# Planning VectorE and GpSimd as engines that take turns, with one set of lengths for all stages

## The chip, the cores and the metric

The kernel runs on one core of a Trainium2 chip. The metric is the device time of one launch in microseconds, as the median of several runs. The core's engines work side by side, each through its own queue in program order: TensorE (PE: matmuls, with weight loads shown apart as PEld), VectorE (DVE), ScalarE (ACT), GpSimd (POOL), and SyncE (SP), which here issues most of the DMAs. An instruction that waits holds up all that stands behind it in its queue.

## The reference, cut to what matters

```python
# attention through 32 landmarks (4 x 8 heads, 576 tokens, 64 wide), then two feed-forward blocks
a = softmax(phi, axis=2)
k_m, v_m = a^T k, a^T v                      # einsum bhsm,bhsd->bhmd
attn = softmax(q k_m^T / 8); x = attn v_m    # heads side by side: 2304 x 512
x = ((x @ moe_w_a) * (x @ moe_w_b)) @ moe_w_out      # 512 -> 1536 -> 512
h = x @ moe2_w_in                                    # 512 -> 2048
out = (h * sigmoid(1.702 h)) @ moe2_w_out            # 2048 -> 512
```

All in 32 bits, to be met closely: `q` and `k` are scaled up, so the softmaxes are sharp.

## The kernel before, in words

**Precision.** Large operands are split into a high part, rounded by ScalarE to a matmul type (L349), and a low part, the difference (L343); each product is three matmul passes. This split is `hi_lo` (L346), and its subtraction goes through `combine` (L339), which also makes the sums and differences below. A `combine` has both inputs in SBUF and may run on VectorE or GpSimd. Evacuations of a PSUM bank have one input in PSUM and run on VectorE or ScalarE. The weights come as 64-bit floats and are decoded in place: two ScalarE passes (L445, L449) and one VectorE operation (L451).

**Stages**, by the trace. 0 to 105 us: attention (`memory`, `queries`, `softmax`), in which `warm_up` and `fill` keep PE running with matmuls of the identity (L1605) where the plan has nothing for it. Then, mixed with it and on to 240 us, `fold` multiplies the first block's weights with the landmark values (L798; out through ACT L818 and DVE L820 into `eff`), and `gated` makes the product of two matmul groups (L852; out through ACT L873 and DVE L876); `sum_tokens` (L892) prepares sums of it on GpSimd alone. 240 to 373 us: `project`, the product with `moe_w_out` as seven products instead of eight: for each of three thirds of the tokens and each product, three operands are loaded, split (128x768, into a ring of three slots) and used by 12 matmuls (L1014); a product's end goes out through DVE L1055. For the next stage `combine_tokens` and `combine_weights` then make seven operands from four (`seven`: four sums, seven splits; 384 and 256 wide). 373 to 548 us: `quad`, the seven products with `moe2_w_in` (L1290, out through DVE L1332). 548 to 592 us: `proj2`, the first 512 tokens with `moe2_w_out` (L1499), for which 16 parts of activations (512 wide, six slots) and the weights are split; beside it `load_pair` fetches eight pairs of weight tiles, issued from ScalarE's queue (L1462), and makes sums of them (256 wide). From 592 us: `proj2_seven`, the other tokens as seven products (L1530).

**What sets the order.** The program is written out by a planner, `Order` (L98). Streams ask for an engine with a ready time and a length in ns; the planner keeps a clock for each engine, and gives the engine to the stream that can start first, in steps of 40 ns, by priority among equals. Where two engines are offered, `_plan` takes the one that ends first, after adding a handicap: 300 for VectorE (`W0`, L22), so GpSimd gets an operation unless VectorE would end over 300 ns sooner. The lengths come from `dve`, `act`, `pool` (L79 to L88) and from the class `Lengths`, whose values are changed by stage: `measured` after the attention, `crowded` from `project` on (there a `combine` counts 1.3 times on GpSimd, 1.75 times on VectorE), `calm` and `short` later. Nothing of this runs on the chip: the lengths decide only in which order each queue's instructions stand, and on which engine.

## Time and profile before

| | us |
|---|---|
| median of 3 runs (740.36, 742.17, 742.63) | 742.17 |
| profiled execution: time, span | 740.76, 739.0 |
| PE busy in the span | 729.0 (99%) |
| VectorE, ScalarE, GpSimd busy | 535.2, 437.9, 294.1 |
| granted TensorE clock | 1.000 |

PE is almost never idle, so the time is the sum of PE's work and its few waits. For each wait one asks which engine ended it. A busy share of VectorE or GpSimd matters only in a stretch where PE waits for them.

### The profile page before, as it was taken

Reading aid. Unit: us, or ns where it says so; the run is one execution under the profiler, and the core shown is the slowest. Engines: PE = TensorE matmul, PEld = TensorE weight load, DVE = VectorE, ACT = ScalarE, POOL = GpSimd, SP = SyncE. Lnnn points to the kernel's source line nnn. Section 1 sums busy time; section 2 is a strip of 40 time slices with the busy share of each in tenths; the row PEclk is TensorE's granted clock in tenths of the full one; section 3 lists DMA queues with packets and bytes.
Section 4 is the critical chain, followed back from the end, with each engine's and each line's share of the span. In section 5 each row is a group of like instructions: output and inputs, shape, how many; then the busy total and the mean of one; then the engine's idle time right before and its main releaser. Section 6 shows DMA issues by size and latency. Waiting matters only on the chain.

```text
span 739.0 us, 14874 instructions
## 1 busy us (share of the span) xinstructions
PE 729.0 (99%) x5480; PEld 687.0 (93%) x5480; DVE 535.2 (72%) x910; ACT 437.9 (59%) x852; POOL 294.1 (40%) x278
## 2 busy tenths in 40 slices
PE   9999999999999999999999999999999999999997
PEld 8877888888889999999999999999998889999997
DVE  3988786568983447945999666676657988888774
ACT  3877664677873447547867676666555564444441
POOL 0414376458896616824998343233250000000000
PEclk9999999999999999999999999999999999999999
DMA  8999854886688875676536888875597474444411
GB/s 269 333 342 298 293 200 153 260 282 218 227 257 281 283 203 165 177 207 190 200 114 203 278 251 267 269 258 186 190 298 244 158 233 137 125 144 144 143 30 29
DMA packets 112600, 157.74 MB, mean 213 GB/s; under 512 B 8592, under 2 KB 89232, under 8 KB 112528
## 3 DMA queue, kind: packets, MB, share of 16 engines
q1 hardware_dynamic: 107168, 147.32, 62.8%
q10 hardware_dynamic: 5360, 9.47, 3.7%
q8 instruction: 43, 0.70, 0.4%
q14 instruction: 29, 0.24, 0.1%
HBM read 104.20 MB, written 52.56 MB: 212 GB/s over the span
## 4 chain that ended last, share of the span: by engine, by line
PE 89%; DVE 4%; DMA 4%; issue 1%; ACT 1%; SPq 0%; POOLq 0%; ACTq 0%; POOL 0%; DVEq 0%
PE bank L1290 22%; PE bank L852 21%; PE bank L1530 19%; PE bank L1014 16%; PE bank L798 3%; DMA raw<-w2d 3%; PE bank L1605 2%; PE bank L596 1%; DMA acc<-g2d 1%; DVE attn L343 1%; PE bank L514 1%; DVE w L343 1%; DVE acc L343 1%; PE bank L635 1%; PE bank L576 0%
## 5 line engine op out<-in xcount | busy, mean ns | idle before, releaser
L852 PEld LDWEIGHTS bank<-attn,eff 128*128 128x128 f32 x1152 | 154.2, 188 | 15.4 <-issue 5.2
L852 PE MATMUL bank<-attn,eff 128*128 128x288 f32 x1152 | 162.8, 298 | 0.0
L349 ACT ACTIVATE w<-acc 128x512 fp32r<-128x512 f32 (+2 forms) x144 | 83.9, 591 | 76.9 <-PE bank L1530 47.8
L1332 DVE TENSOR_TENSOR acc<-bank,acc 128x384 f32<-128x384 f32 x168 | 89.4, 552 | 46.4 <-PE bank L1290 30.9
L343 DVE TENSOR_TENSOR w<-acc,w 128x512 fp32r<-128x512 f32 (+2 forms) x122 | 83.0, 685 | 26.3 <-ACT w L349 26.0
L349 ACT ACTIVATE attn<-acc 128x768 fp32r<-128x768 f32 (+2 forms) x84 | 62.6, 752 | 54.9 <-PE bank L1014 38.9
L1014 PE MATMUL bank<-attn,w 128*128 128x384 f32 x504 | 91.9, 335 | 0.7 <-DVE attn L343 0.7
L343 DVE TENSOR_TENSOR attn<-acc,attn 128x768 fp32r<-128x768 f32 (+2 forms) x61 | 67.1, 1111 | 31.9 <-ACT attn L349 30.7
L1014 PEld LDWEIGHTS bank<-attn,w 128*128 128x128 f32 x504 | 87.6, 188 | 2.0 <-DVE attn L343 1.4
L1342 ACT ACTIVATE acc<-acc 128x384 f32<-128x384 f32 x96 | 48.4, 522 | 26.5 <-DVE acc L1332 25.7
L343 DVE TENSOR_TENSOR acc<-acc 128x512 f32<-128x512 f32 (+2 forms) x90 | 60.8, 686 | 0.8 <-POOL w1b L343 0.5
L1290 PE MATMUL bank<-attn,w 128*128 128x384 f32 x288 | 55.1, 334 | 0.0
L896 POOL TENSOR_TENSOR gr<-gr 128x288 f32<-128x288 f32 x48 | 44.2, 922 | 18.7 <-DMA g1d<-gr 8.2
L343 POOL TENSOR_TENSOR attn<-acc,attn 128x768 fp32r<-128x768 f32 (+1 forms) x22 | 37.7, 1726 | 34.6 <-ACT attn L349 34.6
L343 POOL TENSOR_TENSOR w<-dm,w 128x256 fp32r<-128x256 f32 x35 | 30.8, 894 | 51.2 <-ACT w L349 51.1
L1530 PE MATMUL bank<-attn,w 128*128 128x256 f32 x336 | 50.0, 284 | 1.0 <-ACT w L349 0.7
L1290 PEld LDWEIGHTS bank<-attn,w 128*128 128x128 f32 x288 | 50.4, 188 | 0.0
L1014 PE MATMUL bank<-attn,w1b 128*128 128x384 f32 x252 | 47.6, 336 | 0.2 <-DVE attn L343 0.2
L1290 PE MATMUL bank<-w1b,w 128*128 128x384 f32 x224 | 46.2, 334 | 0.0
L1530 PEld LDWEIGHTS bank<-attn,w 128*128 128x128 f32 x336 | 44.5, 192 | 1.4 <-ACT w L349 1.0
L1014 PEld LDWEIGHTS bank<-attn,w1b 128*128 128x128 f32 x252 | 43.9, 188 | 0.9 <-DVE attn L343 0.5
L1290 PE MATMUL bank<-w 128*128 128x384 f32 x224 | 43.8, 334 | 0.0
(172 smaller groups left out, 1374.7 us busy)
## 6 DMA issues: line engine op xcount, KB each, us to landing
acc<-g1d SPq DMA_DIRECT2D x63, 384.0 KB, 3.7
g2d<-acc SPq DMA_DIRECT2D x96, 192.0 KB, 4.1
acc<-g2d SPq DMA_DIRECT2D x14, 1024.0 KB, 6.4
raw<-in_moe_w_out_dram SPq DMA_DIRECT2D x24, 512.0 KB, 4.9
raw<-in_moe_w_in_dram SPq DMA_DIRECT2D x16, 512.0 KB, 5.1
g1d<-gr SPq DMA_DIRECT2D x12, 576.0 KB, 5.3
g1d<-acc SPq DMA_DIRECT2D x8, 576.0 KB, 4.8
raw<-in_moe_w_a_dram SPq DMA_DIRECT2D x16, 256.0 KB, 4.2
```

The costliest lines, as they stand in the source:

```text
L343: (nc.gpsimd if e == POOL else nc.vector).tensor_tensor(out=dst, in0=in0, in1=in1, op=op)
L349: nc.scalar.activation(out=hi, in_=src, func=AF.Copy)
L514: nc.tensor.transpose(ps[0][:, i * P:(i + 1) * P], qs[0][:, 2 * (c0 + i):2 * (c0 + i) + 2, :].rearrange("p e d -> p (e d)"), ident,)
L798: nc.tensor.matmul(ps[c][0][row(h), :], bdv[b][half, h, :], wt["wab", g, h][0][half, :], start=True, stop=True)
L852: nc.tensor.matmul(dst[:, :U], e[:, c, sw, i * CW + j * P:i * CW + (j + 1) * P], attn(b, mv, c, u * U, U), start=(n == 0), stop=(n == 3 * ...
L896: nc.gpsimd.tensor_tensor(out=dst, in0=in0, in1=in1, op=ALU.subtract)
L1014: nc.tensor.matmul(ps[0][:, :N2], w1_of(a, g, sw)[:, r * P:(r + 1) * P], b[0][:, mv, i], start=(first and q == n == 0), stop=(q == NG1 // ...
L1290: nc.tensor.matmul(ps[0][:, :N2], w[:, sw, r, :], y[mv][r], start=(n == 0), stop=(n == 5))
L1332: nc.vector.tensor_tensor(out=s[0], in0=ps[0][:, :N2], in1=x[0], op=ALU.add)
L1342: nc.scalar.activation(out=c[0], in_=c[0], func=AF.Gelu_apprx_sigmoid)
L1530: nc.tensor.matmul(ps[name][0][:, :NB], x[0][:, sw, c, :], moving(b, h // 2 + c, mv), start=(h == c == n == 0), stop=(h > 0 and c == K4 - ...
L1605: nc.tensor.matmul(ps[0][:, :P], ident, ident, start=True, stop=True)
```

## The change

The planner's model is replaced. `Lengths` and all that set it go (`measured`, `crowded`, `short`, `calm`); `dve` and `act` become fixed sums, 72 + n/0.96 and 100 (or 56 from PSUM) + n/1.2. A length may be marked `Held`: the planner keeps one more clock, `port`, and an operation with a `Held` length starts no earlier than the last `Held` one ended, on either engine. `Held` are both choices of `combine`, the decoding step L451, the GpSimd copy L545 and `sum_tokens`. The handicap for VectorE is -300 instead of 300. In the front part the planner reckons with loads at 335 bytes/ns that land 1700 ns later (300 and 2500 before), and with 110 ns instead of 70 for some transposes. The arithmetic is unchanged.

```diff
-W0 = 300.0
+W0 = -300.0
...
-FRONT = 1.0, 1.0, 1.0
-RATE0 = 300.0, 2500.0
+RATE0 = 335.0, 1700.0
...
+SIX = 798.0
...
-class Lengths:
-    dve, act, psum = 68, 94, 52
-    six, wide, three = 740, 2.54, 650
-    pool, both, slow = 1.0, 1.0, 1.0
...
-def measured():
-    Lengths.dve, Lengths.act, Lengths.psum = 150, 205, 160
-    Lengths.six, Lengths.wide, Lengths.three = 795, 2.71, 690
-    Lengths.pool, Lengths.both, Lengths.slow = 1.15, 1.4, 1.15
...
-def crowded():
-    measured()
-    Lengths.pool, Lengths.both, Lengths.slow = 1.3, 1.75, 1.55
...
-def dve(n, fast=False):
-    return Lengths.dve + n / (1.92 if fast else 0.96)
+class Held(float):
+
+    pass
+
+
+def dve(n):
+    return 72 + n / 0.96
 
 
 def act(n, psum=False):
-    return (Lengths.psum if psum else Lengths.act) + n / 1.2
+    return (56 if psum else 100) + n / 1.2
...
-        self.clock = {PE: 0.0, ACT: 0.0, DVE: 0.0, POOL: 0.0}
-        self.dma, self.marks, self.streams, self.count = 2000.0, {}, [], 0
+        self.clock, self.port = {PE: 0.0, ACT: 0.0, DVE: 0.0, POOL: 0.0}, 0.0
+        self.dma, self.marks, self.streams, self.count = 2800.0, {}, [], 0
...
-            t = max(self.clock[e], r[1])
+            t = max(self.clock[e], r[1], self.port if isinstance(d, Held) else 0.0)
...
             self.clock[e] = t + d
+            if isinstance(d, Held):
+                self.port = t + d
...
-        both = {POOL: Lengths.pool * pool(n), DVE: Lengths.both * dve(n)}
+        both = {POOL: Held(pool(n)), DVE: Held(dve(n))}
...
-        t, _ = yield DVE, t, slow * dve(512)
+        t, _ = yield DVE, t, Held(dve(512))
...
-            t, e = yield {POOL: 900, ACT: act(HG * C0 * M)}, max(t, et[1])
+            t, e = yield {POOL: Held(700), ACT: act(HG * C0 * M)}, max(t, et[1])
...
-            t, _ = yield POOL, t, Lengths.pool * pool(U)
+            t, _ = yield POOL, t, Held(pool(U))
```

**What it does to the queues.** The operations on PE, ScalarE and the DMA queues stay the same in kind, but for the identity matmuls L1605 (63 before, 56 now) eight small evacuations that go from ScalarE to VectorE, and two pairs of `gated` evacuations that are merged. Of the 530 `combine` operations 358 stood on VectorE and 172 on GpSimd; now it is 491 and 39. `sum_tokens` (96 operations) stays on GpSimd. In what follows the changed kernel's lines count lower: L328 is the old L343, L319 the old L334, L435 the old L451, L803 the old L820, L334 and L1435 on ScalarE the old L349 and L1462.

VectorE in `project`, at the second third of the tokens, before (`attn_83<-acc` is the split of an operand that PE waits for, 768 wide; `eff` and `acc`, 384 wide, are `combine_tokens` for the next stage):

```order
L343 TENSOR_TENSOR attn_83<-acc,attn_83 128x768 x4
L343 TENSOR_TENSOR acc<-acc 128x384
L343 TENSOR_TENSOR attn_83<-acc,attn_83 128x768 x2
L343 TENSOR_TENSOR acc<-acc 128x384 x2
L343 TENSOR_TENSOR eff<-acc,eff 128x384
L343 TENSOR_TENSOR attn_83<-acc,attn_83 128x768 x2
L343 TENSOR_TENSOR eff<-acc,eff 128x384
L343 TENSOR_TENSOR attn_83<-acc,attn_83 128x768 x3
```

Beside it GpSimd, before:

```order
L343 TENSOR_TENSOR eff<-acc,eff 128x384
L343 TENSOR_TENSOR acc<-acc 128x384
L343 TENSOR_TENSOR eff<-acc,eff 128x384 x2
L343 TENSOR_TENSOR acc<-acc 128x384
L343 TENSOR_TENSOR eff<-acc,eff 128x384
L343 TENSOR_TENSOR attn_83<-acc,attn_83 128x768
L343 TENSOR_TENSOR acc<-acc 128x384
```

The same place on VectorE now:

```order
L328 TENSOR_TENSOR attn_83<-acc,attn_83 128x768 x3
L328 TENSOR_TENSOR eff<-acc,eff 128x384 x2
L328 TENSOR_TENSOR acc<-acc 128x384
L328 TENSOR_TENSOR attn_83<-acc,attn_83 128x768
L328 TENSOR_TENSOR acc<-acc 128x384
L328 TENSOR_TENSOR eff<-acc,eff 128x384
L328 TENSOR_TENSOR attn_83<-acc,attn_83 128x768
L328 TENSOR_TENSOR acc<-acc 128x384
L328 TENSOR_TENSOR eff<-acc,eff 128x384
L328 TENSOR_TENSOR attn_83<-acc,attn_83 128x768
```

All 22 operations of that `combine_tokens` pair now stand on VectorE, two or three after each 768-wide split, and GpSimd has none of them.

VectorE in the attention, around the first `eff` evacuation, before (`sT` and `aT` are attention scores, `mx` and `sm` their small statistics):

```order
L343 TENSOR_TENSOR sT_112<-sT_112,sm_116 128x288
L676 STREAM_TRANSPOSE aT<-sT_112 128x288
L820 TENSOR_TENSOR eff<-bank,eff 128x512 x2
L676 STREAM_TRANSPOSE aT<-sT_111 128x288
L665 TENSOR_REDUCE sm_117<-sT_112 128x9
L562 TENSOR_REDUCE mx_106<-bank 128x1
```

The same place now:

```order
L328 TENSOR_TENSOR sT_112<-sT_112,sm_117 128x288
L328 TENSOR_TENSOR sT_112<-sT_112,sm_116 128x288
L328 TENSOR_TENSOR sT_111<-sT_111,sm_115 128x288
L660 STREAM_TRANSPOSE aT<-sT_112 128x288
L803 TENSOR_TENSOR eff<-bank,eff 128x512 x2
L328 TENSOR_TENSOR attn_83<-aT,attn_83 128x288
L660 STREAM_TRANSPOSE aT<-sT_111 128x288
L649 TENSOR_REDUCE sm_117<-sT_112 128x9
L546 TENSOR_REDUCE mx_106<-bank 128x1
```

Three operations that GpSimd had have joined VectorE's row.

ScalarE near the end of `proj2`, before (`w_1709<-acc 128x512` is a split of activations, the last of the 16 parts the one ahead of the row of six; the 256-wide rows are pairs of weights; L1462 issues a pair's load and waits until its buffer is free):

```order
L349 ACTIVATE w_1709<-acc 128x512
L1462 DMA acc<-w2d 128x2x512
L349 ACTIVATE w_1709<-raw_74 128x256 x3
L349 ACTIVATE w_1709<-acc 128x512
L349 ACTIVATE w_1709<-acc 128x256
L1462 DMA acc<-w2d 128x2x512
L349 ACTIVATE w_1709<-acc 128x256
L349 ACTIVATE w_1709<-acc 128x512
L349 ACTIVATE w_1709<-acc 128x256 x6
```

The same place now:

```order
L334 ACTIVATE w_1639<-acc 128x256 x4
L334 ACTIVATE w_1639<-acc 128x512
L1435 DMA raw_73<-w2d 128x2x512
L1435 DMA raw_74<-w2d 128x2x512
L334 ACTIVATE w_1639<-acc 128x512
L334 ACTIVATE w_1639<-raw_73 128x256 x2
L334 ACTIVATE w_1639<-acc 128x512
L334 ACTIVATE w_1639<-raw_73 128x256 x2
L334 ACTIVATE w_1639<-raw_74 128x256 x4
```

The eight pair loads now go to `acc`, `raw`, `acc`, `raw` by twos (before: `acc`, `acc`, `raw`, `acc`), and the last two are issued together, ahead of the last two splits of activations.

## Rows read from the trace of the kernel before

**Rows 1.** The page: the span, and part 1 for PE.

```profile
span 739.0 us, 14874 instructions
PE 729.0 (99%) x5480; PEld 687.0 (93%) x5480; DVE 535.2 (72%) x910; ACT 437.9 (59%) x852; POOL 294.1 (40%) x278
```

**Rows 2.** Busy time by stretch: stretch, length, engines, granted clock, DMA share, GB/s.

```profile
0.00:30.00 30.00, 28.64 (x365) 24.90 (x366) 17.56 (x52) 15.56 (x37) 4.40 (x11) 1.00 0.88 293
30.00:60.00 30.00, 27.51 (x316) 22.60 (x316) 26.48 (x60) 24.14 (x55) 9.48 (x11) 1.00 0.99 329
...
284.00:302.00 18.00, 17.56 (x99) 16.73 (x98) 17.27 (x12) 12.87 (x24) 17.42 (x12) 1.00 0.55 156
...
352.00:374.00 22.00, 21.49 (x123) 20.85 (x122) 21.43 (x21) 15.27 (x30) 22.00 (x17) 1.00 0.47 164
374.00:541.00 167.00, 167.00 (x965) 167.00 (x964) 121.95 (x213) 114.54 (x240) 78.49 (x86) 1.00 0.72 231
541.00:600.00 59.00, 57.81 (x287) 49.34 (x286) 44.56 (x102) 32.98 (x73) 6.59 (x5) 1.00 0.72 233
600.00:739.00 139.00, 135.03 (x1126) 134.83 (x1124) 107.25 (x193) 58.36 (x96) 0.00 (x0) 1.00 0.38 115
```

**Rows 3.** Timeline: start, length, instruction, in brackets idle time before and its releaser.

```profile
43.45 1.07 PE L514 MATMUL bank<-ident,q 128*128 128x128 f32 x8 [0.76 <-DMA q<-in_q_dram]
...
59.74 0.33 PE L514 MATMUL bank<-ident,q 128*128 128x128 f32 x1 [1.18 <-ACT qT L332]
...
296.64 4.11 PE L1014 MATMUL bank<-attn,w 128*128 128x384 f32 x22 [0.23 <-DVE attn L343]
...
301.31 0.98 PE L1014 MATMUL bank<-attn,w1b 128*128 128x384 f32 x4 [0.21 <-DVE attn L343]
...
366.90 0.65 PEld L1014 LDWEIGHTS bank<-attn,w 128*128 128x128 f32 x4 [0.81 <-DVE attn L343]
366.90 0.81 PE L1014 MATMUL bank<-attn,w 128*128 128x384 f32 x3 [0.49 <-DVE attn L343]
...
594.61 0.50 PE L1530 MATMUL bank<-attn,w 128*128 128x256 f32 x2 [0.75 <-ACT w L349]
```

**Rows 4.** VectorE's groups, 241 to 279 us, GpSimd mostly idle: count, busy us, mean ns.

```profile
L343 DVE TENSOR_TENSOR attn<-acc,attn 128x768 fp32r<-128x768 f32 x15 | 14.9, 993 | 14.2 <-ACT attn L349 13.8
L1055 DVE TENSOR_TENSOR acc<-bank,gr 128x384 f32<-128x384 f32 x6 | 3.3, 557 | 5.9 <-PE bank L1014 5.9
```

**Rows 5.** The same for 284 to 306 us, VectorE and then GpSimd.

```profile
L343 DVE TENSOR_TENSOR attn<-acc,attn 128x768 fp32r<-128x768 f32 x9 | 14.9, 1686 | 2.1 <-ACT attn L349 2.1
...
L343 POOL TENSOR_TENSOR eff<-acc,eff 128x384 fp32r<-128x384 f32 x6 | 8.8, 1478 | 5.6 <-ACT eff L349 5.6
```

**Rows 6.** Timeline: single operations with the other engine idle, and two back to back.

```profile
283.41 1.02 POOL L343 TENSOR_TENSOR eff<-acc,eff 128x384 fp32r<-128x384 f32 x1 [5.64 <-ACT eff L349]
...
294.34 0.55 DVE L343 TENSOR_TENSOR eff<-acc,eff 128x384 fp32r<-128x384 f32 x1
...
591.67 1.29 DVE L343 TENSOR_TENSOR w<-acc,w 128x512 fp32r<-128x512 f32 x2 [1.00 <-ACT w L349]
```

**Rows 7.** VectorE's groups, 352 to 374 us, and two of 30 to 60 us.

```profile
L1055 DVE TENSOR_TENSOR acc<-bank,gr 128x384 f32<-128x384 f32 x6 | 3.2, 550 | 0.6 <-PE bank L1014 0.6
...
L876 DVE TENSOR_TENSOR gr<-bank,gr 128x288 f32<-128x288 f32 x8 | 3.6, 454 | 2.4 <-PE bank L852 2.0 <-ACT raw_p L449 0.3
...
L343 DVE TENSOR_TENSOR attn<-aT,attn 128x576 fp32r<-128x576 f32 x1 | 0.7, 747 | 0.0
```

**Rows 8.** ScalarE's timeline, the chain of waits, the landing of L1462's loads.

```profile
583.22 0.37 ACTq L1462 DMA_DIRECT2D acc<-w2d  x1
583.63 1.55 ACT L349 ACTIVATE w<-acc 128x256 fp32r<-128x256 f32 x4 [1.05 <-DVE acc L343]
...
585.78 8.12 DMA acc<-g2d
...
DMA to landing us min/median/max: 3.6/4.7/7.3
```

More of the change, by code (lines that the diff above doesn't have):

```diff
@@ L54 @@
 )
-class Lengths:
-    dve, act, psum = 68, 94, 52
-    six, wide, three = 740, 2.54, 650
-    pool, both, slow = 1.0, 1.0, 1.0
-def measured():
-    Lengths.dve, Lengths.act, Lengths.psum = 150, 205, 160
-    Lengths.six, Lengths.wide, Lengths.three = 795, 2.71, 690
-    Lengths.pool, Lengths.both, Lengths.slow = 1.15, 1.4, 1.15
-def crowded():
-    measured()
-    Lengths.pool, Lengths.both, Lengths.slow = 1.3, 1.75, 1.55
-def short():
-    Lengths.dve, Lengths.act, Lengths.psum = 68, 94, 52
-    Lengths.pool, Lengths.both, Lengths.slow = 1.0, 1.0, 1.0
-def dve(n, fast=False):
-    return Lengths.dve + n / (1.92 if fast else 0.96)
+class Held(float):
+    pass
+def dve(n):
+    return 72 + n / 0.96
 def act(n, psum=False):
-    return (Lengths.psum if psum else Lengths.act) + n / 1.2
+    return (56 if psum else 100) + n / 1.2
 def pool(n):
@@ L168, in _plan @@
         if not isinstance(r[0], dict):
-            t = max(self.clock[r[0]], r[1] + (70.0 if r[0] == PE else 0.0))
+            t = max(self.clock[r[0]], r[1] + (70.0 if r[0] == PE else 0.0), self.port if isinstance(r[2], Held) else 0.0)
             return (t if len(r) < 4 else max(t, min(x[1] for x in r[3].free))), r[0], r[2]
@@ L441, in decode_piece @@
         mu = mf.bitcast(U32)
-        slow = Lengths.slow
         t, _ = yield ACT, t, act(512)
@@ L547, in memory @@
                 nc.scalar.activation(out=dst, in_=src, func=AF.Copy)
-        part = 240 if n < NHG else 70
+        part = 240 if n < NHG else 110
         t, ba = yield PE, t, part * last, bank_a
@@ L572, in memory @@
         nc.scalar.activation(out=et[0][:, last, :, 0], in_=even, func=AF.Exp, bias=m[2], accum_out=m[4])
-        t, _ = yield PE, t, 70 * last
+        t, _ = yield PE, t, 110 * last
         for c in range(last):
@@ L578, in memory @@
             )
-        t1, _ = yield PE, t2, 70
+        t1, _ = yield PE, t2, 110
         nc.tensor.transpose(bb[0][:, P:2 * P], et[0][:, last].rearrange("p s x -> p (s x)"), ident)
@@ L737, in close_attention @@
         pa.release()
-        measured()
         nonlocal py, pw
@@ L840, in gated @@
                 if not wide:
-                    t, ps = yield PE, t0, Lengths.six, bank_m
+                    t, ps = yield PE, t0, SIX, bank_m
                     dst = ps[0]
                 elif j == 0:
-                    t, ps = yield PE, t0, Lengths.six, pair_s
+                    t, ps = yield PE, t0, SIX, pair_s
                     dst = ps[0][:, j]
                 else:
-                    t, _ = yield PE, t0, Lengths.six
+                    t, _ = yield PE, t0, SIX
                     dst = ps[0][:, j]
@@ L1147, in room_kept @@
         give(f_s, views(acc, FN, 3, 2 * AN))
-    def calm():
-        for p in (1, 2):
-            for r in range(2):
-                yield "mark", "yc", p, r
-        measured()
     def room_projected():
-        od.spawn(9, calm())
         nonlocal p2
@@ L1176, in room_last @@
     def room_last():
-        short()
         alone[0] = True
@@ L1210, in room_last @@
             yield "mark", "wt", p
-        short()
         give(fw_s, views(acc, 2 * FN, 1))
@@ L1610, in main @@
         room_gated()
-        crowded()
         for p in range(NP):
@@ L1644, in tile_mem_attention_moe_moe2 @@
         n0 = 2 * NHG
-        measured()
-        Lengths.pool, Lengths.both, Lengths.slow = FRONT
         def loads():
```

## The prediction

> **What bounds the kernel now.** The page comes first: PE is busy for 729.0 of 739.0 us [rows 1], at the full granted clock in every stretch [rows 2]. PE's instructions stay as they are, so the change can move the time only by the 10 us in which PE is idle, by the identity matmuls that fill the front, and by waits that it adds. The table by stretch says where the idle time lies [rows 2]: 1.36 us in the first 30, 2.49 in 30 to 60, 0.44 in 284 to 302, 0.51 in 352 to 374, 1.19 in 541 to 600, and 3.97 at the very end, behind the last matmul. These add up to the 10 us, so from 60 to 284 and from 374 to 541 there is none: what VectorE does there is hidden, whichever engine has it. PE's timeline then names the releasers [rows 3]. In the front they are a load (0.76) and a ScalarE evacuation (1.18). In `project` all three are VectorE's 768-wide split (0.23, 0.21, 0.49). Near 594 us it is a ScalarE split (0.75).
>
> **Part 1: combines go from GpSimd to VectorE in `project`.** While GpSimd is mostly idle, a 768-wide split takes VectorE 993 ns [rows 4]; where GpSimd runs `combine_tokens` beside it, 1686 ns [rows 5]. So an operation that GpSimd takes over costs VectorE 0.69 us all the same, and done by VectorE itself it takes 0.55 us (384 wide, alone) [rows 6]. GpSimd needs 1.48 us for it there, 1.02 alone [rows 5, 6]. An evacuation from PSUM is not slowed: 550 ns in a stretch where GpSimd never rests, 557 where it does [rows 4, 7]. In these stretches GpSimd is no help to VectorE, and the two hold up the splits on which PE waits.
>
> Does VectorE alone keep up? In 284 to 306 us it would have nine splits (9 x 0.993 = 8.9 us) and the 22 operations of one `combine_tokens` pair (22 x 0.55 = 12.1): 21.0 us of 22. Back to back it is less: between 0.55 at 384 and 0.993 at 768 a 512-wide one lies at 0.70, yet two take 1.29 [rows 6], so 0.1 us of each overlaps the next; 31 operations then take 18 us. PE needs 12 matmuls at 167.00/965 = 0.173 us [rows 2] for each split, 2.08 us, or 18.7 us for nine, and the ring of three slots lets a split be up to two steps (4 us) early. It fits by the one count and nearly by the other, with two or three short operations between splits instead of one long one. I take these waits as gone. Their size: PE's idle time is 0.23 + 0.21 + 0.49 = 0.93 us, but the end of a pipelined matmul is modelled; the weight load before the third shows 0.81 instead of 0.49, 0.32 more, which for three gives 1.9. I take the middle, **-1.4 us**, with bounds -1.9 and 0.
>
> In 352 to 374 us, with the pairs of `combine_weights` beside the splits, both engines are full now: 21.43 and 22.00 of 22 us [rows 2]. VectorE alone: its own work without the six evacuations, (21.43 - 3.2) x 993/1686 = 10.7; the evacuations 3.2 [rows 7]; GpSimd's at 0.55 for 1.48 us, 8.2. That is 22.1 us of 22, or 18.3 with 0.1 of overlap for each of 38 operations. This is the tightest place of the change, and part of this work may run later, under `quad`, where VectorE is busy for 121.95 of 167 us [rows 2].
>
> A rule of the Trainium skill speaks against the move: Perfetto Trace Analysis, "Optimizing Scalar/DVE Operations", says that if VectorE is saturated, giving some of its work to other engines, even GpSimd, may make sense, and adds that the read port these two share may undo that. In this stretch the trace bears out the second half (993 against 1686 ns); by the first half the sum would hold +1 to +2 us here in place of the gain, and that is the slower rival below.
>
> **Part 2: the front.** Between the first and the third pair of `eff` evacuations VectorE gets four operations more of 288 columns and three of 576. Alone these take about 0.45 and 0.75 us [rows 7]: 4.0 us, less 0.7 of overlap 3.3. Evacuations that change places with ScalarE there about cancel (two wide ones fewer, four narrow ones more). VectorE has 30 - 26.48 = 3.5 us idle in 30 to 60 us [rows 2]: the work just fits, if the idle time lies where it is wanted. PE's waits there were ended by a load and by ScalarE, neither of which moves up much; the queue's new order may shift them. Bounds: -2.5 (all idle time closes) and +3.3 (none of VectorE's idle time can be used). I take **+0.2 us**, near the middle, since VectorE's new work meets its idle time. The seven identity matmuls fewer are worth nothing: they stand before the first `fold`, which waits for loads and decoding on ScalarE, and idle time takes their place.
>
> **Part 3: the end of `proj2`.** The chain of waits runs here through the last split of activations, which frees the buffer for a load of 8.12 us issued behind it (585.78), whose split is what PE waits for at 594.61 [rows 3, 8]. That split stood in ScalarE's queue behind the load of the last weight pair (L1462, issued at 583.22) and a 256-wide operation after 1.05 us of idle time [rows 8]. Now the last two pair loads are issued together, earlier, and the middle ones go to the raw buffers, so that they need not wait until the pairs before them are done with `acc`. Against it, two splits of the pair just loaded stand ahead of the last one, and such a load takes 3.6 to 7.3 us to land [rows 8]; before, too, the last but one pair stood so. If the last split comes 1.2 us earlier, PE's idle time of 1.19 us is gone [rows 2]; nothing more is to be had, because PE's own stream is late next. I take **-1.1 us**; bounds -1.2 and +2.6 (a pair load that takes the longest 7.3 us instead of the median 4.7).
>
> **Parts at nothing.** The fixed lengths and the load rates act only through the order. In `quad` VectorE gets most of GpSimd's 78.49 us [rows 2], at 0.55/1.48 of it some 29 us, less than its 45 us of idle time, and its evacuations from PSUM keep first claim by priority. If that cover were gone, each late evacuation would cost PE 0.55 us. In `gated` the sums stay on GpSimd.
>
> **Sum.** -1.4 + 0.2 - 1.1 = -2.3 us. Against the profiled execution's 740.76 that gives 738.5. This execution lies 1.4 us under the median of the three runs; carried over to the median, 742.17 - 2.3 = **739.9 us**. About 0.3%, 2.2 us, is what a measurement of this kernel can tell from no change, so the forecast lies on that edge.
>
> **The rivals.**
> - *The front closes too.* With ScalarE relieved of small evacuations its chain comes earlier, and PE's 2.49 us go as well: -1.4 - 2.5 - 1.1 = -5.0, 737.2 us. For it: 1.18 of the 2.49 us are ended by ScalarE [rows 3]. Against: the load at 43.45 has its own time.
> - *Gains and losses cancel.* VectorE, full in 30 to 60 us, delivers `eff` and scores about 1.5 us later, and the pair load lands late enough that the end of `proj2` gains little: -1.4 + 1.5 - 0.3 = -0.2, 742.0 us. For it: 3.3 us of work against 3.5 us of scattered idle time.
> - *VectorE becomes the bound* (slower). One mechanism, in 284 to 374 us and once in the front: the row of operations on VectorE is longer than PE's matmuls need, and GpSimd stands idle. It decides where VectorE's sum passes the stretch: 22.1 of 22 us by durations is that point, 18.3 by overlap is well below. Price: up to 22.1 + two late splits of 0.99 in 22 us is +2, and +3.3 in the front less what its idle time still takes, say +1.5: +3.5 in all with the end of `proj2` unchanged, 745.7 us. The rule named above is this case. Against it: in 284 to 302 us, where the trace has the two engines together, the same work takes longer than VectorE alone would need.
> - *The change doesn't act*: the order shows that it does, 133 combines change engine. That the turns are no turns is excluded by 993 against 1686.
>
> **How the numbers follow.** Forecast 0.45, the front closes too 0.15, cancel 0.25, VectorE the bound 0.15. Of the forecast's 0.45 two thirds lie beyond the 2.2 us, since its own bounds reach further down than up: 0.31 faster, 0.14 same. With 0.15 of the first rival, faster is 0.46; same 0.14 + 0.24 = 0.38; slower 0.15 + 0.01 = 0.16. The range takes in the first rival (737.2, less the 0.7 to the bound of part 1 and the rest of part 3: 736.5) and the lower part of the slower one: 744.3.
>
> **What would show it.** Right: no PE wait on the 768-wide split from 284 to 374 us; that split near 1.0 us there with GpSimd idle; VectorE's busy time higher in 30 to 60 and 284 to 374 us with PE's not lower; the last activation split ended before 583 us and no wait of PE behind 592 us. Wrong: PE waiting for VectorE between 352 and 400 us, or for `eff` or scores before 105 us, or ScalarE waiting for the last pair's load longer than 1.05 us.

## The result and the profile after

The changed kernel takes 745.68 us (median of 5 runs, 742.45 to 746.60); the kernel before, timed beside it, 740.50. The ratio is 1.0059, 95% interval 1.0038 to 1.0081; timed again later it was 1.0080 (1.0058 to 1.0102). So it is slower, by 4.4 and 5.9 us by the two ratios, which is small but clear of 1 by both intervals. Forecast was 739.9, with a range up to 744.3.

In code lines, the changed kernel's L328 and L334 are before's L343 and L349 (the two halves of a split), L781 and L835 its L798 and L852 (fold and gated), L997 its L1014 (projection), L1019 its L1036 (the copy that evacuates a product), L958 and L880 its L975 and L897 (loads of activations, stores of the gated sums), L1503 its L1530 (last stage).

Where did the time go? PE's instructions are the same except for seven identity matmuls, though in the front in another order, so the starts of its stages say it at once (us; two profiles of each kernel, the second ones from the experiments below):

| from the first matmul of ... to that of the next | before | before, again | after | after, again |
|---|---|---|---|---|
| start of the span to gated | 30.77 | 31.25 | 30.62 | 30.18 |
| gated (with attention and folds) | 208.77 | 208.87 | 211.51 | 213.26 |
| project | 133.72 | 133.75 | 135.75 | 135.35 |
| quad | 174.72 | 174.72 | 174.72 | 174.72 |
| proj2 | 43.71 | 43.56 | 43.56 | 43.56 |
| proj2_seven to the end | 147.29 | 146.97 | 147.73 | 148.52 |
| span | 738.98 | 739.12 | 743.89 | 745.59 |

Of the 4.9 us between the first profiles 2.74 arise in the gated stage and 2.03 in the projection. The quads, in which GpSimd's busy time falls from 78.49 [rows 2] to 25.65 us, agree to 0.01 us.

How much of it is waiting? PE's busy time over the gated stage before and after, then over the projection before and after (length, then PE, PEld, VectorE, ScalarE, GpSimd, clock, DMA share, GB/s):

```profile
30.77:239.54 208.77, 206.28 (x1980) 178.64 (x1979) 153.57 (x266) 138.01 (x281) 124.54 (x120) 1.00 0.78 257
30.62:242.13 211.51, 208.30 (x1981) 178.26 (x1979) 167.58 (x293) 137.39 (x277) 94.66 (x97) 1.00 0.77 256
239.54:373.26 133.72, 132.77 (x759) 130.91 (x758) 88.78 (x85) 77.12 (x125) 78.59 (x58) 1.00 0.66 199
242.13:377.88 135.75, 133.44 (x759) 132.51 (x757) 91.75 (x139) 77.83 (x127) 9.34 (x9) 0.99 0.67 197
```

In the gated stage PE's idle time grows by only 0.72 us (2.49 to 3.21); its busy time, for the same matmuls at the full clock, grows by 2.02. The page, and what PE waited for, by engine, tile and line, with the sum, the count and the longest wait in us (answers to [rows 1] and [rows 3]):

```profile
span 743.9 us, 14800 instructions
PE 730.1 (98%) x5466; PEld 686.1 (92%) x5466; DVE 563.4 (76%) x1049; ACT 431.8 (58%) x842; POOL 139.5 (19%) x145
```

```profile
PE bank L560 <- ACT et L552: 2.7, 2, 2.2
PE bank L997 <- ACT attn L334: 1.7, 1, 1.7
...
PE bank L1503 <- ACT w L334: 1.4, 1, 1.4
PE bank L541 <- DMA phi<-in_phi_dram: 0.7, 1, 0.7
PE bank L835 <- DVE eff L803: 0.4, 1, 0.4
```

The stretches of [rows 2], with 60 to 105 us added, and VectorE's 768-wide split and 384-wide operation in 284 to 306 us, which answer [rows 5] and [rows 6]:

```profile
30.00:60.00 30.00, 27.91 (x310) 21.66 (x309) 28.42 (x69) 23.04 (x52) 3.80 (x4) 1.00 0.97 321
60.00:105.00 45.00, 43.88 (x531) 36.08 (x531) 39.70 (x89) 31.27 (x78) 16.99 (x19) 1.00 0.82 274
284.00:302.00 18.00, 17.82 (x103) 17.86 (x104) 14.67 (x25) 13.78 (x26) 0.00 (x0) 1.00 0.64 180
...
352.00:374.00 22.00, 22.00 (x129) 22.00 (x128) 20.74 (x37) 18.16 (x34) 1.23 (x1) 1.00 0.71 225
374.00:541.00 167.00, 167.00 (x966) 167.00 (x965) 132.43 (x268) 109.94 (x236) 25.65 (x26) 1.00 0.67 223
```

```profile
L328 DVE TENSOR_TENSOR attn<-acc,attn 128x768 fp32r<-128x768 f32 x10 | 9.5, 954 | 3.0 <-ACT attn L334 2.7
L328 DVE TENSOR_TENSOR eff<-acc,eff 128x384 fp32r<-128x384 f32 x8 | 4.3, 551 | 0.3 <-ACT eff L334 0.3
```

So where the change was aimed at it does what it says: GpSimd is empty from 284 to 352 us, the split takes 954 ns instead of 1686, VectorE has 3.3 us to spare in 284 to 302 us, and PE's waits for it there are gone but for 0.2 us. The losses are elsewhere, at three places.

**261 us, in the projection.** The chain of waits (start, length, what) with ScalarE's timeline around it (start, length, instruction, in brackets idle time and its releaser):

```profile
254.44 0.36 SPq L958
...
254.89 6.46 DMA g1d<-gr
...
261.85 0.84 ACT attn L334
262.71 0.97 DVE attn L328
```

```profile
255.41 0.47 ACT L1019 ACTIVATE gr<-bank 128x384 f32<-128x384 f32 x1
261.46 0.49 ACT L1019 ACTIVATE gr<-bank 128x384 f32<-128x384 f32 x1 [5.58 <-DMA g1d<-gr]
```

ScalarE stands for 5.58 us at a copy into the storage "gr", until the store of the last gated block's sums, which reads that storage, has landed. The store was issued only at 254.89, behind a load on SP that waited for room, and took 6.46 us. Behind the copy, in ScalarE's queue, stand the splits that PE needs: it waits 1.70 us, then 0.37 for VectorE. Before, SP's last such store read another buffer:

```profile
251.32 0.36 SPq L897 DMA_DIRECT2D g1d<-acc  x1
```

Then the granted clock falls (PE alone: length, busy, clock, DMA share, GB/s):

```profile
260.00:262.00 2.00, 1.04 (x6) 1.00 0.49 182
262.00:264.00 2.00, 0.89 (x3) 1.00 0.00 0
264.00:266.00 2.00, 2.00 (x8) 0.55 0.51 135
266.00:268.00 2.00, 2.00 (x8) 0.59 0.99 313
268.00:270.00 2.00, 2.00 (x13) 1.00 0.63 175
```

After the idle time in 260 to 264 us PE runs for some 3.4 us at the lower level (0.50, 1.2 GHz), which loses 1.7 us more (0.45 and 0.41 of 2 us each): the waits of 2.07 us cost nearly twice their length. The first experiment has the sum.

**59 us, in the front.** The end of the chain of waits there, then PE's timeline around it, after and before:

```profile
57.99 0.68 DVE sT L328
58.70 0.68 ACT sT L647
59.38 0.97 ACT eff L801 x2
60.35 0.68 ACT et L552 x2
61.08 0.66 PE bank L560 x4
```

```profile
58.27 0.66 PE L498 MATMUL bank<-ident,q 128*128 128x128 f32 x4
61.08 0.66 PE L560 MATMUL bank<-ident,et 128*128 128x128 f32 x4 [2.16 <-ACT et L552]
```

```profile
59.83 2.62 PE L852 MATMUL bank<-attn,eff 128*128 128x288 f32 x18
...
62.83 0.60 PE L576 MATMUL bank<-ident,et 128*128 128x128 f32 x4
```

PE waits 2.16 us for ScalarE's exponential "et" (the longest wait there before is 1.18, for another evacuation [rows 3]). It stands in ScalarE's queue behind the exponential "sT", and that one waits for a subtraction on VectorE (57.99) which GpSimd did before. But "et" is not late: before, ScalarE began "sT" at 58.52 us instead of 58.70, and "et" at 61.21 instead of 60.24:

```profile
61.21 0.68 ACT L568 ACTIVATE et<-bank,mx 128x512 f32<-128x512 f32 x1
```

What differs is PE's own order. Before, PE had done 114 gated matmuls when it came to the transposes of "et" (L576, now L560), at 62.83 us and without a wait; now 96, so 18 that had covered the exponential stand behind it.

Before 105 us PE's gaps behind its first matmul add up to 4.21 us instead of 2.49; 0.7 of them in the first profile is a late load of phi. And PE's work is cut finer: 84 of the 1152 gated matmuls start 180 ns or more before the next (68 before), mostly 215 to 240 ns against 133 in a run, some 1.4 us of the 2.02 us of busy time above. The seven identity matmuls fewer are 1.1 us less of PE's work.

**599 us, ahead of the last stage.** PE waits 1.35 and 0.22 us: the last load of activations goes out 0.7 us earlier against PE than before (6.64 us ahead of the stage's first matmul, 5.91 before) but takes 8.87 us instead of 8.12 [rows 8]:

```profile
589.52 8.87 DMA acc<-g2d
```

### The profile page after: what moved, and what is told of

Its sections match the earlier page's. It is cut to its first block, busy times and chain, and to the rows that moved or that the text cites. A ratio compares the mean times of both kernels' runs of the same rounds, so it can differ in the third digit from the quotient of the medians.

```text
span 743.9 us, 14800 instructions
## 1 busy us (share of the span) xinstructions
PE 730.1 (98%) x5466; PEld 686.1 (92%) x5466; DVE 563.4 (76%) x1049; ACT 431.8 (58%) x842; POOL 139.5 (19%) x145
## 4 chain that ended last, share of the span: by engine, by line
PE 91%; DVE 4%; DMA 3%; ACT 1%; issue 1%; ACTq 0%; SPq 0%
PE bank L1263 23%; PE bank L835 21%; PE bank L1503 19%; PE bank L997 16%; PE bank L781 3%; PE bank L1472 3%; PE bank L580 1%; PE bank L1578 1%; DMA acc<-g2d 1%; PE bank L498 1%; DMA kv<-in_k_dram 1%; DMA g1d<-gr 1%; DVE w L328 1%; PE bank L619 1%; DVE attn L328 0%
## 5 line engine op out<-in xcount | busy, mean ns | idle before, releaser
L835 PEld LDWEIGHTS bank<-attn,eff 128*128 128x128 f32 x1152 | 154.4, 188 | 17.1 <-issue 6.0
L835 PE MATMUL bank<-attn,eff 128*128 128x288 f32 x1152 | 165.0, 298 | 0.4 <-DVE eff L803 0.4
L334 ACT ACTIVATE w<-acc 128x512 fp32r<-128x512 f32 (+2 forms) x142 | 82.7, 593 | 75.3 <-PE bank L1503 42.2
L328 DVE TENSOR_TENSOR w<-acc,w 128x512 fp32r<-128x512 f32 (+2 forms) x135 | 86.6, 648 | 27.2 <-ACT w L334 26.3
L328 DVE TENSOR_TENSOR attn<-acc,attn 128x768 fp32r<-128x768 f32 (+2 forms) x75 | 66.3, 896 | 38.5 <-ACT attn L334 37.5
L997 PE MATMUL bank<-attn,w 128*128 128x384 f32 x504 | 92.8, 339 | 2.3 <-ACT attn L334 1.7
L997 PEld LDWEIGHTS bank<-attn,w 128*128 128x128 f32 x504 | 89.1, 191 | 3.2 <-ACT attn L334 2.0
L334 ACT ACTIVATE attn<-acc 128x768 fp32r<-128x768 f32 (+2 forms) x80 | 61.0, 769 | 48.3 <-PE bank L997 42.4
L328 DVE TENSOR_TENSOR acc<-acc 128x512 f32<-128x512 f32 (+2 forms) x100 | 60.4, 624 | 0.1
L879 POOL TENSOR_TENSOR gr<-gr 128x288 f32<-128x288 f32 x52 | 49.4, 951 | 45.7 <-DMA g1d<-gr 21.4
L1503 PE MATMUL bank<-attn,w 128*128 128x256 f32 x336 | 50.0, 284 | 1.6 <-ACT w L334 1.4
L997 PE MATMUL bank<-attn,w1b 128*128 128x384 f32 x252 | 47.1, 334 | 0.0
L1503 PEld LDWEIGHTS bank<-attn,w 128*128 128x128 f32 x336 | 44.5, 192 | 2.0 <-ACT w L334 1.6
L997 PEld LDWEIGHTS bank<-attn,w1b 128*128 128x128 f32 x252 | 44.0, 188 | 0.0
L1503 PE MATMUL bank<-w 128*128 128x256 f32 x294 | 41.0, 283 | 0.0
L1263 PEld LDWEIGHTS bank<-w1b,w 128*128 128x128 f32 x224 | 39.5, 188 | 0.0
```

The source lines that it names most:

```text
L328: (nc.gpsimd if e == POOL else nc.vector).tensor_tensor(out=dst, in0=in0, in1=in1, op=op)
L334: nc.scalar.activation(out=hi, in_=src, func=AF.Copy)
L835: nc.tensor.matmul(dst[:, :U], e[:, c, sw, i * CW + j * P:i * CW + (j + 1) * P], attn(b, mv, c, u * U, U), start=(n == 0), stop=(n == 3 * ...
L879: nc.gpsimd.tensor_tensor(out=dst, in0=in0, in1=in1, op=ALU.subtract)
L997: nc.tensor.matmul(ps[0][:, :N2], w1_of(a, g, sw)[:, r * P:(r + 1) * P], b[0][:, mv, i], start=(first and q == n == 0), stop=(q == NG1 // ...
L1263: nc.tensor.matmul(ps[0][:, :N2], w[:, sw, r, :], y[mv][r], start=(n == 0), stop=(n == 5))
```

## The experiments

Kernels named a_ start from the changed kernel, those named b_ from the kernel before. Each one's median, its ratio to the kernel before, and its stages in us; "front" is first gated to first projection matmul (before 208.77, after 211.51).

| kernel | median | ratio (95%) | front | project | quad | span |
|---|---|---|---|---|---|---|
| a_place | 742.94 | 1.0035 (1.0015, 1.0055) | 214.14 | 131.57 | 174.72 | 740.25 |
| a_w0 | 752.73 | 1.0150 (1.0122, 1.0179) | 213.53 | 133.63 | 177.93 | 749.92 |
| a_noturn | 760.36 | 1.0255 (1.0230, 1.0280) | 217.22 | 142.89 | 176.86 | 759.14 |
| a_rate | 748.91 | 1.0093 (1.0074, 1.0113) | 218.73 | 131.55 | 174.72 | 747.13 |
| b_late | 745.12 | 1.0059 (1.0040, 1.0078) | 208.75 | 132.23 | 177.67 | 744.12 |
| b_w0 | 749.10 | 1.0122 (1.0101, 1.0142) | 214.03 | 132.33 | 178.62 | 748.15 |
| b_rate | 747.64 | 1.0102 (1.0084, 1.0120) | 210.30 | 136.76 | 174.78 | 744.74 |
| b_plain | 772.91 | 1.0437 (1.0411, 1.0464) | 227.25 | 139.35 | 182.23 | 770.70 |
| a_et | 743.93 | 1.0031 (1.0016, 1.0045) | 214.01 | 131.52 | 174.72 | 741.76 |
| a_again | 747.27 | 1.0080 (1.0058, 1.0102) | 213.26 | 135.35 | 174.72 | 745.59 |
| b_again | 740.91 (one run) | - | 208.87 | 133.75 | 174.72 | 739.12 |
| b_join | 739.81 | 0.9985 (0.9970, 1.0001) | 208.76 | 131.56 | 174.72 | 735.53 |
| b_join2 | 739.30 | 0.9975 (0.9963, 0.9987) | 208.74 | 131.57 | 174.72 | 737.69 |
| a_back | 752.27 | 1.0158 (1.0135, 1.0181) | 212.87 | 138.65 | 175.11 | 750.61 |

**a_place: other storage for the copies, same order.**

```
-        give(hc_s, views(p2_m, N2, 7))
+        give(hc_s, [views(p2_m, N2, 7)[i] for i in (0, 5, 6, 1, 2, 3, 4)])
```

> The changed kernel, with one difference: the seven 384-wide pieces of storage that the projection's copies use are handed out in the order 0, 5, 6, 1, 2, 3, 4, so that the second copy no longer goes where the last gated block's sums are still being stored. Order of instructions on every engine unchanged. Theory (the store holds the copy, the copy holds ScalarE, ScalarE holds TensorE, and the lower clock follows the wait): the projection gets 4.2 us shorter (first projection matmul to first quad matmul 135.75 us in the changed kernel, 131.5 here), no granted clock under 1.00 at 264 to 268 us, span near 739.7 us, ratio to the kernel before 1.000. Rival (the wait only shows where VectorE or the loads are late): TensorE waits again within 10 us, projection 134 to 136 us, ratio 1.004 to 1.006.

The projection took 131.57 us, 4.18 less (2.07 of waits, 1.7 of slow clock, 0.4 of PE's busy time besides), with the clock at 1.00 from 256 to 284 us: the wait for the store and what follows it are the whole loss there, and without them the projection is 2.15 us shorter than before:

```profile
244.76:376.33 131.57, 131.34 (x759) 131.05 (x758) 91.95 (x139) 78.16 (x127) 7.67 (x8) 1.00 0.67 199
```

The span is 0.5 us off what was expected, the ratio 0.0035. A part of that comes from the front, where this time the clock fell. PE's timeline and the clock there:

```profile
62.03 0.66 PE L560 MATMUL bank<-ident,et 128*128 128x128 f32 x4 [2.50 <-ACT et L552]
```

```profile
62.00:64.00 2.00, 1.97 (x12) 0.73 0.89 257
64.00:66.00 2.00, 2.00 (x10) 0.50 0.82 223
66.00:68.00 2.00, 2.00 (x46) 0.92 1.07 385
```

The order is that of the changed kernel, whose wait of 2.16 us left the clock at 1.00. Of a_place's ten runs four have a mean granted clock of 0.999 or more (741.39 to 742.89 us) and six 0.992 to 0.997 (742.03 to 748.01): the wait at 59 us lies where the clock falls in some executions and not in others. But the four at the full clock have a median of 742.5 us, still 1.6 above the kernel before beside them (740.88): the rest is the front's loss without a fall of the clock.

**a_w0, a_noturn, a_rate: one part of the change undone each** (preference; turns; arrival numbers).

```
-W0 = -300.0
+W0 = 300.0
```

```
-            if isinstance(d, Held):
-                self.port = t + d
```

```
-RATE0 = 335.0, 1700.0
+RATE0 = 300.0, 2500.0
...
-        part = 240 if n < NHG else 110
+        part = 240 if n < NHG else 70
```

> The changed kernel with the preference undone (W0 300 instead of -300, so that GpSimd takes more of the two-operand work); turns, plain lengths and arrival rates stay. If the preference for VectorE made the front longer (first gated matmul to first projection matmul 208.8 us before, 211.5 after), it is near 209 here and the span near 741; if turns or rates did, it stays near 211.5. The projection's wait for the store may go or stay, since the order of the gated blocks' buffers is drawn anew: projection 131.5 to 136 us. Ratio 0.998 to 1.006.

> The changed kernel without the turns (VectorE and GpSimd reckoned free of each other); preference, plain lengths and arrival rates stay. If turns made the front longer, first gated matmul to first projection matmul goes from 211.5 to about 209 us; if the preference or the rates did, it stays near 211.5. Where GpSimd gets work back, VectorE's 768-wide split beside it is long again (993 ns alone in the kernel before, 1686 beside), and TensorE waits for it again between 284 and 374 us, 0.9 us in all as in the kernel before. Ratio 0.998 to 1.006.

> The changed kernel with the arrival rates of before (RATE0 300 and 2500, first transfer at 2000, and 70 instead of 110 for a transpose); turns, plain lengths and preference stay. If the arrival numbers made the front longer, first gated matmul to first projection matmul goes from 211.5 to about 209 us and the 2.2 us that TensorE waits for an exponential at 58.9 us goes; if VectorE's load did, both stay. Ratio 0.998 to 1.006.

None brings the front back to 209 us; each makes it longer, by 2.0, 5.7 and 7.2 us. So no single part carries the front's loss: each undone part gives a new order with waits of its own. Two things can be read nevertheless. The store's wait at the first copies comes and goes with the order of the front: it holds ScalarE 5.0 us in a_w0 and 7.4 in a_noturn (PE waits 1.1 and 3.6 there), and it is not there in a_rate, whose projection takes 131.55 us. The clock fell behind the wait of 3.6 us in a_noturn (266.6 us) and behind one of 2.2 in a_rate's front (48.4), and not behind the 1.1 us of a_w0. And without turns PE waits for VectorE again in the projection, more than expected; its waits there:

```profile
PE bank L995 <- ACT attn L332: 3.6, 1, 3.6
PE bank L995 <- DVE attn L326: 3.5, 4, 1.9
```

**b_w0, b_rate, b_plain: one part done alone, from the kernel before** (the same lines the other way; for b_plain the three functions that set longer lengths do nothing).

> The kernel before with the preference alone (W0 -300 instead of 300). If preferring VectorE costs the front its 2.6 us, the first projection matmul comes at about 242 us instead of 239.5; if it does so only together with the rest, it stays within 1 us of 239.5. In the projection the reckoned prices of that stage (VectorE at 1.75) outweigh 300 ns, so some splits stay on GpSimd: projection 132 to 134 us. Ratio 0.998 to 1.006.

> The kernel before with the arrival numbers of the change alone (RATE0 335 and 1700, first transfer at 2800, 110 for a transpose). If these make the front later by themselves, the first projection matmul comes at about 242 us instead of 239.5; else within 1 us of 239.5. Projection about 133.7 us as before, unless the gated blocks' buffers come out in another order and the first copies meet the last store there (then 136 to 138). Ratio 0.998 to 1.008.

> The kernel before with plain lengths in all stages (72, 100 and 56 ns fixed, no factors), but no turns, no preference, and the arrival numbers of before. VectorE and GpSimd are then planned as if they did not disturb each other, while the trace of before shows the 768-wide split at 993 ns alone and 1686 beside GpSimd. If turns are what plain lengths need, the projection and the quads get waits for VectorE or GpSimd: projection 135 us or more, quads over 174.72 us, ratio over 1.005; if not, both stay, ratio 0.997 to 1.003.

All three are slower. b_w0's front is 5.3 us longer (1.7 of them from a fall of the clock at 62.7). b_rate's projection of 136.76 us lies in the range put down for copies that meet the last store, but not by that cause: ScalarE doesn't wait for the store there, and PE waits 2.9 us for GpSimd's splits and 1.4 for VectorE's. b_plain is the clearest: with plain lengths and no turns, PE waits for VectorE in folds, gated products, projection and quads:

```profile
PE bank L1010 <- DVE attn L339: 5.8, 5, 2.0
PE bank L848 <- DVE eff L816: 4.9, 6, 1.8
PE bank L1286 <- DVE acc L1328: 4.2, 6, 1.2
```

So plain lengths don't do without the turns (a_noturn says the same, at 1.0255). That the longer lengths of before were a rough way to the same end is a reading, which no run tests.

**b_late: only the projection's splits moved, in the kernel before.**

```
-        crowded()
+        crowded(); od.handicap[DVE] = -5000.0
         for p in range(NP):
             yield from project(p)
-        yield from quad(*order[0])
+        od.handicap[DVE] = W0; yield from quad(*order[0])
```

> The kernel before with one difference: during the projection alone (240 to 373 us) every split goes to VectorE; front, quads and tail are planned by the numbers of before, and TensorE's own order is that of before. Theory (of the change, the projection's part brings a gain by itself): the projection takes 131.6 us instead of 133.71, TensorE waits less than 0.3 us in it, the front stays at 239.5 us, span near 736.9 us, ratio 0.997. Rival (VectorE becomes the bound once it has all splits): waits for VectorE of over 1 us between 284 and 374 us, projection 134 us or more, ratio 1.000 or more.

The projection gained 1.5 us, as the theory had it, and VectorE did not become the bound. But the quads lost 2.95, more than that (PE waits 0.9 us for ScalarE and 0.9 for GpSimd in them, at another order), and the first gated matmul came 2.5 us late although the order up to there is that of before: phi's second transfer landed at 6.71 us instead of 4.77. PE's second row in that profile, beside that of b_again:

```profile
6.85 2.36 PE L557 MATMUL bank<-ident,phi 128*32 128x128 f32 x40 [1.29 <-DMA phi<-in_phi_dram]
```

```profile
5.50 2.11 PE L557 MATMUL bank<-ident,phi 128*32 128x128 f32 x40
```

**a_et: the wait at 59 us taken away.** On top of a_place, the exponential "sT" is planned behind "et":

```
-        t, _ = yield ACT, t, act(w)
+        t, _ = yield ACT, max(t, (yield "mark", "exp", 4)) if n == 3 else t, act(w)
```

> The changed kernel with the projection's storage handed out as in a_place, and one more difference: ScalarE's exponential for a block of scores (sT, at 58.7 us) is planned behind the exponential of phi's fifth block (et, at 60.2 us), for which TensorE waited 2.2 us in the changed kernel and 2.5 us in a_place. Theory (TensorE waits there because of ScalarE's order alone): the wait at 59 us falls to 0.5 us or less, no granted clock under 1.00 at 62 to 67 us, first projection matmul near 240 us (242.13 in the changed kernel, 244.76 in a_place), span near 736 to 738 us, ratio 0.995 to 0.999. Rival (VectorE, without a pause from 42 to 55 us, is late for what comes next): the wait moves on to the next scores or folds within 10 us, first projection matmul at 242 us or later, ratio 1.000 or more.

The wait shrank to 0.51 us and the clock stayed at 1.00, but the first projection matmul came at 244.10 us, as the rival had it. The rival's reason, VectorE, is not shown: from 60 us to the first projection matmul PE waits 0.4 us for VectorE and 2.4 for ScalarE, and PE's busy time in the gated stage is 210.32 us, 4.0 above before. A wait of 1.48 us has appeared at 144 us, where ScalarE decodes a piece that has just been loaded ahead of a gated evacuation; PE's and ScalarE's timelines:

```profile
144.64 1.60 PE L835 MATMUL bank<-attn,eff 128*128 128x288 f32 x10 [1.48 <-ACT acc L856]
```

```profile
142.84 0.66 ACT L429 ACTIVATE spare<-raw 128x512 f32<-128x512 f32 x1 [2.56 <-DMA raw<-in_moe_w_b_dram]
...
143.96 0.63 ACT L856 ACTIVATE acc<-bank 128x576 f32<-128x576 f32 x1
```

With the storage of a_place and this the kernel is 1.0031 (1.0016 to 1.0045): both waits gone, and still not under the kernel before.

**a_again, b_again: both kernels once more.**

> The changed kernel, unchanged, profiled and timed once more. By the theory the wait for the store at 261 us is there again, with about 4 us of granted clock at 0.50 to 0.69 behind it (projection 135.7 us). The wait at 59 us was 2.2 us without a fall of the clock in the first profile and 2.5 us with one in a_place: here either, the first projection matmul at 242 or at 244 to 245 us. Ratio 1.004 to 1.008.

> The kernel before, unchanged, profiled once more. What differs between its two profiles is the chip's own spread: if the second transfer of phi (landed at 4.77 us in the first profile, 6.71 in the kernel with the projection alone moved) is late here too, the first fold comes at 28 to 29.6 us instead of 27.14 and the front is up to 2.5 us longer with the same instructions; if not, the stages agree within 0.3 us, span 739.

The kernel before repeats within 0.6 us in every stage, with the same waits. The changed one has all its waits again, and this time the clock fell at both: at the end of 2.5 us at 59 us and behind 1.3 and 0.4 at 262.

**b_join, b_join2, a_back: front and back exchanged.** b_join is the kernel before with the change's turns, plain lengths and preference switched on ahead of the first projection matmul; a_back is the changed kernel with the numbers of before from there. PE's order is that of the kernel whose front it has. In b_join's edit, plain() sets 72, 100 and 56 ns without factors for all that follows and switches the turns on:

```
+        plain()
+        od.handicap[DVE] = -300.0
         room_gated()
-        crowded()
```

> The kernel before up to the first projection matmul (every engine's order there as before), and from there the change's reckoning: turns, plain lengths, VectorE preferred. TensorE's order is that of before all through. Theory (the change is a gain behind the front, and its loss lies in the front and in one wait for a store): front 239.5 us, projection 131.6 to 132.2 us, quads 174.7, then 43.6 and 141.3 to 143.4; span 735 to 737.5, ratio 0.994 to 0.998. Rival (the back of the changed kernel only fits its own front): waits in the quads as in the kernel with the projection alone moved (quads 177.67 us there), span 740 us or more, ratio 1.000 or more.

> The counterpart of b_join: the changed kernel up to the first projection matmul (every engine's order there as changed), and from there the reckoning of before (the longer lengths, no turns, GpSimd preferred). TensorE's order is the changed kernel's. If the change's front loses by itself, the first projection matmul comes at 242 to 244.8 us again; if its back gains by itself, this kernel also loses what b_join won there: projection 133 us or more with waits for VectorE between 284 and 374 us, quads 174.7 or more; span 743 to 750, ratio 1.005 to 1.012. If the wait for the store at 261 us comes from where the front leaves its buffers, it may be here too (projection 135.7 us or more, the clock down behind it); if it comes from the order in which loads and that store are issued behind the front, it is gone, since here the store stands ahead of the load. Rival (front and back gain or lose only as a pair): front within 1 us of 239.5, or projection near 131.6.

> The kernel b_join (front of before, reckoning of the change behind it) profiled and timed once more, over more rounds. Its first profile had a span of 735.5 us and its timed runs a median of 739.8 us. If the gain behind the front is steady (projection 131.56, quads 174.72, 43.56 and 141.97 us in the first profile) and only the front and the wait ahead of the last stage vary, those four stages come out within 1.5 us in sum here, and the ratio is 0.996 to 0.999. Rival: some runs have a wait in the quads or a fall of the clock, which the first profile did not show; then the quads exceed 174.8 us here or the ratio is 1.000 or more.

These four corners say which half loses:

| | back of before | back of the change |
|---|---|---|
| front of before | 1 | 0.9985 (0.9970, 1.0001), 0.9975 (0.9963, 0.9987) |
| front of the change | 1.0158 (1.0135, 1.0181) | 1.0059 (1.0038, 1.0081), 1.0080 (1.0058, 1.0102) |

The front loses by itself (212.87 us in a_back, 1.7 of them from a fall of the clock), and the back gains by itself: the projection is 131.56 and 131.57 us, 2.15 under before, with quads at 174.72. In a_back ScalarE stands for 4.81 us at the same copy, so the wait for the store comes from where the front leaves its buffers. Its projection has the old waits and more, VectorE's split at 1446 ns beside GpSimd in 284 to 306 us:

```profile
260.07 0.49 ACT L1055 ACTIVATE gr<-bank 128x384 f32<-128x384 f32 x1 [4.81 <-DMA g1d<-gr]
```

```profile
PE bank L1033 <- POOL attn L362: 2.9, 3, 1.5
PE bank L1033 <- DVE attn L362: 1.7, 3, 0.8
```

b_join2's two middle stages repeat b_join's, but proj2 and the last stage are 2.1 us longer in sum, more than the 1.5 expected: PE waits 1.3 us for ScalarE's "w" ahead of the last stage, which b_join did not. The two don't add up: behind the front of the change its own back is 5 to 7 us better than the old one, behind the old front 1 to 2. By the second ratio the kernel that joins the old front to the new back is faster than the kernel before, by 0.13 to 0.37%, and so than both.

## Why the prediction was wrong

**Part 1, the projection: right in mechanism, a little short in size.** -1.4 us was put down, with -1.9 as its bound; without the store's wait it is -2.15 (131.57 against 133.72). VectorE alone kept up: 14.67 us of 18 in 284 to 302 us and 20.74 of 22 in 352 to 374, against the 18.3 to 22.1 that the prediction reckoned for the second. Two thirds of the gain is not idle time in the profile: in a_place PE's idle time in the projection falls by 0.72 us against before and its busy time by 1.43, which the prediction had suspected when it put the bound at -1.9. The 0.55 us of [rows 6] was not read alone, since GpSimd ran beside that operation from 294.50 us; with GpSimd empty it is 551 ns, so the term stands. The rule of the Trainium skill weighed there (Perfetto Trace Analysis, "Optimizing Scalar/DVE Operations", that giving VectorE's work to other engines may help when it is saturated, unless the shared port undoes it) is borne out in its second half again: 954 ns with GpSimd empty, 1446 with it busy in a_back.

**The step that failed first is one that was not made: the sum held no term for buffers.** The prediction followed operations between engines and looked for waits of PE on VectorE in 284 to 374 us. The 4.2 us came at 261 us, from a copy on ScalarE behind a store, because the reordered front leaves its last sums in the storage that the projection's first copies overwrite. a_place, which changes only that storage, shows it. It stood in the order of instructions, in the name of the buffer in SP's last store. With it the term of the projection is +2.0 instead of -1.4.

**Part 2, the front: the place was named, the step was wrong.** +0.2 was taken between -2.5 and +3.3; measured is +2.6 from the start to the first projection matmul (242.13 against 239.54), +3.9 in the second profile, +5.2 in a_place, in both of which the clock fell. The prediction reckoned this stretch by VectorE ("the work just fits") and held that PE's time can move only by its idle time, the identity matmuls and waits that are added. VectorE's busy time did rise, 26.48 to 28.42 us in 30 to 60, but that is not what the largest wait shows: the exponential came earlier than before, and PE's new order came to it earlier still. And most of the stage's 2.74 us is none of the three terms: the same matmuls in a finer cut kept PE busy 2.02 us longer. By the profiles, whose matmul ends are modelled, this share is in all runs of that front (208.3 us, and 207.9 to 208.6 in a_again, a_back and a_place less 1.7 for the clock, against 206.3 to 206.6 with the old front). That the seven identity matmuls are worth nothing held: PE spends 1.1 us less on them, and the first gated matmul comes only 0.15 us earlier.

**Part 3, the end of proj2: -1.1 was wrong, it is +0.3 here and +1.6 in the second profile.** The load did go out earlier, by 0.7 us, but took longer by 0.75. Over the profiles it takes 7.8 to 9.3 us, and PE's wait behind it varies from 0 (a_place) to 2.1 us (a_again). The same kernel differs in its last two stages by 0.8 us (changed) and 2.1 (b_join) from one profile to the next, so the order decides less there than the transfer does.

**Parts at nothing** held in the quads: 132.43 us of VectorE in 167, and 174.72 us to the hundredth. In the gated stage, put at nothing because the sums stay on GpSimd, the loss above arose.

**The rivals.** The slower one gave 745.7 us, the time that was measured, but not by its mechanism: in 284 to 374 us PE hardly waits for VectorE, b_late and b_join exclude it there. That its price met the measured time is luck. Of its terms only the loss in the front, +1.5, came true, larger and by PE's order rather than by VectorE. The sum of what the profiles show is +2.6 + 2.0 + 0.3 = +4.9. Of the "wrong if" list the entry for 352 to 400 us stayed silent, and the one for the front (PE waits for eff at 45 us, 0.38) pointed at the right stretch. The third stood at its mark: ScalarE waits 1.10 us at 586.5 for the first sum of the last two pairs, where 1.05 was named.

**What stays open.** That the changed front is worse is shown as a whole; which part of the change gives PE that order is not. The parts undone one by one, and the largest wait taken away, gave orders with other waits. The profiles divide the loss into waits and a finer cut of PE's work, but no run takes away the finer cut alone.

## What to carry to other kernels

When a planner's numbers change, read from the new order which buffer each stage leaves its last result in and who writes there next, and follow the store that reads it; a busy-time sum doesn't show this. Read TensorE's own order as well: the same matmuls in another order changed both its waits and its busy time. Price a wait of 1.5 to 2.5 us on TensorE at up to twice its length, because of the clock behind it. And test a change of a planner by stages, joining the old order of one stage to the new of another: that kept here a gain of 1 to 2 us, where the change as a whole loses 4 to 6.

## What the runs showed of the hardware

- The granted clock fell to its lower level, 0.50, for some 3.4 us each time, which costs 1.7 us, at the end of a wait of PE or up to 1.3 us behind it: at 1.70 and 0.37 us at 261 us (after), 1.3 and 0.4 there (a_again), 3.6 there (a_noturn), 2.5 at 59 us (a_place, a_again), 2.2 there (a_back), 1.9 there (b_w0), 2.2 at 46 (a_rate) and 2.0 at 603 (a_back). It did not fall behind 2.16 us at 59 (after), nor behind 1.48 at 143 (a_et) or 2.1 at 598 (a_again). So the length of one wait does not settle it.
- A gated matmul starts 133 ns before the next in a run of its kind, and mostly 215 to 240 ns where the run is broken (84 of 1152 in the changed kernel, 68 before): a finer cut of the same work is longer without a wait in the profile.
- The first transfers vary from execution to execution: the one of phi that SP issues at 1.85 us landed between 4.69 (b_join) and 6.89 us (a_noturn). In b_late, at 6.71, it moved all that follows, to the first gated matmul, by 2.5 us against before, with the same order of PE.
